# Eight matmuls on a zeroed tile first, the second chunk's moves on two queues, and the first two key tiles on one

## The chip, the core and the metric

The kernel runs on one core of a Trainium2 chip. The metric is the device time of the program in microseconds (us): before the change the median of three runs is 1068.44 us (1065.55 to 1068.86). Engines are named as in the profile: PE (TensorE matmuls; PEld its weight loads), DVE (VectorE), ACT (ScalarE), POOL (GpSimd), SP (SyncE). A "queue" is an engine that issues DMAs: here SP and ACT do.

## What is computed

An attention layer with talking heads, and two feed-forward layers behind it:

```python
scores = scale * np.matmul(q, k.transpose(0, 1, 3, 2))          # 4 batches, 12 heads, 448 x 448, depth 64
scores = np.einsum('bhij,hg->bgij', scores, w_pre)              # mix of the heads
scores = scores - np.max(scores, axis=-1, keepdims=True)
attn = np.exp(scores)
attn = attn / (np.sum(attn, axis=-1, keepdims=True) + 1e-09)
attn = np.einsum('bhij,hg->bgij', attn, w_post)                 # mix of the heads again
x = np.matmul(attn, v)                                          # then 1792 tokens of 768
h = x @ w_in                                                    # 768 -> 2048, ELU, -> 768
...
h = x @ w_in                                                    # 768 -> 1024, softmax * h, norm, -> 768
```

## The kernel before

The attention is worked off in chunks of query rows. The rows of a batch are cut into chunks of up to 12 groups of ten rows; the first batch has chunks of 6, 6, 12, 12 and 9 groups (`CH`), called chunk 0, 1, 2 and so on here. A chunk passes these steps:

1. **Scores** (`add_half` for chunks 0 and 1, L448; `add_score` for the others, L495): PE multiplies query tiles `q` and key tiles `kt` into PSUM tiles `sc`. One key tile holds two heads, so the six tiles of a batch are numbered by h = 0, 2, ..., 10. In chunks 0 and 1 a group of four matmuls takes two key tiles: h = 0 and 2, then 4 and 6, then 8 and 10.
2. **Evacuation** (`evac`, L454 and L501): ACT or DVE copies `sc` into SBUF: into tiles `s` of their own for chunk 0, into a ring of eight tiles `sev` for the others.
3. **Moves** (`move`, issued at L417): DMAs inside SBUF put the rows of a head into a tile `sp` in which head and row stand as the head mix needs them: ten rows of `sp` per move, for the last head twice five. A chunk has 13 moves. A move carries 105 KB in a chunk of 6 groups and 210 KB in one of 12.
4. **Units** of two groups: `pre` (L572) mixes the heads, out of `sp` into two PSUM tiles `pm` of a ring of three; DVE takes the maximum (L577), ACT the exponential (L582), POOL scales the second mix (L593), and `post` (L605) does the second mix with 56 small matmuls into `po`; a copy goes to `at`.
5. **Times the values** (L654, `av`), in two halves per chunk, and a store.

Units 0 to 2 belong to chunk 0, 3 to 5 to chunk 1, 6 to 11 to chunk 2. The first `pre` of a chunk waits for all 13 moves of it.

The order of the instructions on each engine isn't written out. `op` records every step with a rank (about when it is due, in planned us) and a planned duration for each engine that may do it, and `schedule()` puts the steps in order, engine by engine, and picks the engine for a step that lists several. So a move that lists `sp` and `act` may be issued by either queue, and any change of a rank or a duration can shift steps on all engines up to the end of the attention. Each engine then runs its own list in order: an instruction that waits holds up all behind it, a DMA issue on ACT's list included. All DMAs of both queues share eight semaphores in turn, so that a new one is issued only when the one eight places before it has landed.

Two feed-forward layers follow (from about 350 us on): L260 and L807, then L912 and L979.

Of the kernel before, what the change touches and what calls it, by code (L numbers as in the profile page):

```python
# [9 lines left out]
F32 = mybir.dt.float32  # L10
# [55 lines left out]
def kernel(ctx: ExitStack, tc: tile.TileContext, qa, kt, vt, wpre, wpost,  # L66
# [4 lines left out]
    nc = tc.nc  # L71
# [3 lines left out]
    def pool(name, bufs=1, side="left", space=None):  # L75
        kw = {"space": space} if space is not None else {"side": side}
        p = tc.alloc_tile_pool(name=name, bufs=bufs, reuse_waits="tile", **kw)
        pools[name] = p
        return p
# [48 lines left out]
    const = pool("const")  # L128
# [13 lines left out]
    ps_pm = pool("ps_pm", 3, space=PSUM)  # L142
# [152 lines left out]
    def op(rank, emit, deps=(), new=(), uses=(), more=0.0, lag=None, port=False, **us):  # L295

        o = Op()
        o.port = port
        o.rank, o.emit, o.deps, o.new, o.us, o.more, o.lag = rank, emit, [d for d in deps if d is not None], new, us, more, lag
        for b in chain(new, uses):  # L300
            b.users.append(o)
        ops.append(o)
        return o
# [67 lines left out]
    def copier(e):  # L371
        return nc.scalar.copy if e == "act" else nc.vector.tensor_copy
# [39 lines left out]
    kt_t, kb, q_t, qb_, sp_t, sp_op, pre_op, e_t = {}, {}, {}, {}, {}, {}, {}, {}  # L412
    po_t, ps_t, st_t, wr_t, v_t, x_t, at_t, T = {}, {}, {}, {}, {}, {}, {}, {}
    k_op, q_op, av_op, sc_ev = {}, {}, {}, {}

    def dma(out, in_, e="sp"):
        {"act": nc.scalar, "pool": nc.gpsimd, "sp": nc.sync}[e].dma_start(out=out, in_=in_)  # L417
# [2 lines left out]
    pool("spb")  # L420
    k0 = pool("k0")

    def add_q(c, hf):

        qb_[c, hf] = Buf("q")
        r = t_sc[c, 6 * hf]

        def load(e):
            q_t[c, hf] = q_p.tile([128, 3, 128], F32, tag="q", name="q")
            dma(q_t[c, hf], qa[c, :, 3 * hf:3 * hf + 3])  # L430

        q_op[c, hf] = op(r - 9 if c > 1 else 6.2 if c else [0.0, 3.0][hf], load, [], [qb_[c, hf]], sp=.5, more=.5)

    def add_half(c, n):

        b, _, G = CH[c]
        ring = ("sc", "pm")[n % 2] if c == 0 else "sc"
        scb, svb = [Buf(ring) for _ in range(2)], [Buf("sev") for _ in range(2)]
        r = t_sc[c, 4 * n]
        key = "sc", c, n  # L440

        def mm(e):
            T[key] = [pools["ps_" + ring].tile([128, 512], F32, tag=ring, name="sc") for _ in range(2)]
            q = q_t[c, 0].rearrange("p k n -> p (k n)")
            for x in range(2):
                for i in range(2):
                    sl, o = slice(64 * i, 64 * i + 64), 64 * (2 * n + x)
                    nc.tensor.matmul(T[key][i][64 * x:64 * x + 64, :S], q[sl, o:o + 64], kt_t[b, 4 * n + 2 * x][sl, :],  # L448
                                     start=True, stop=True)

        def evac(e, i):
            t = T["sv", c, n, i] = (k0.tile([128, S], F32, name=f"s0_{n}{i}") if c == 0 else
                                    sev_p.tile([128, S], F32, tag="sev", name="sev"))
            copier(e)(t, T[key][i][:, :S])  # L454

        def move(e, i, x, p, r0, r1):
            dma(sp_t[c][p:p + 13 * (r1 - r0 - 1) + 1:13, 0:G, :], T["sv", c, n, i][64 * x + r0 * G:64 * x + r1 * G], e)

        o1 = op(r, mm, [k_op[b, 4 * n], k_op[b, 4 * n + 2], q_op[c, 0]], scb, [qb_[c, 0], kb[b, 4 * n], kb[b, 4 * n + 2]], pe=SC)
        for i in range(2):  # L460
            sv = [] if c == 0 else [svb[i]]
            o2 = op(r + .9 + .1 * i, lambda e, i=i: evac(e, i), [o1], sv, [scb[i]], act=.43, dve=.54)
            for x in range(2):
                h = 4 * n + 2 * x + i
                for k, to in enumerate([(h, 0, 10)] if h < 11 else [(11, 0, 5), (64, 5, 10)]):
                    sp_op.setdefault(c, []).append(op(r + 2 + .2 * i + .1 * x + .05 * k, lambda e, i=i, x=x, to=to: move(e, i, x, *to),
                                                      [o2, o_clear.get(c)], [spb_[c]], sv, lag=3.5, sp=.78, **({'act': .78} if c == 0 else {})))

    def add_k(b, h):

        kb[b, h] = Buf("k")

        def load(e):
            kt_t[b, h] = k_p.tile([128, S], F32, tag="k", name="kt")
            dma(kt_t[b, h], kt[b, h // 2], e)

        r0 = t_sc[HEAD[b] - 1, h] if b else 0.0
        k_op[b, h] = op(r0 - 4 if b else .5 + h * .1 if h < 8 else 6.0 + h * .01, load, [], [kb[b, h]], lag=3.0, **{"sp" if b or h % 4 == 0 else "act": .5})

    def add_score(c, h):  # L480

# [33 lines left out]
    spb_ = {c: Buf(f"sp{(NC - c) % 3}") for c in range(NC)}  # L515
# [8 lines left out]
    def clear(t, us, r):  # L524
        return op(r, lambda e: nc.gpsimd.memset(t, 0.0), pool=us)
# [3 lines left out]
    o_clear = {c + 3: clear(sp_t[c][:, CH[c][2]:], .38 * (NH - CH[c][2]), 4.0 + c) for c in range(2)}  # L529
# [10 lines left out]
    for c in range(NC):  # L540
        b = CH[c][0]
        if c == HEAD[b]:
            for h in range(0, NH, 2):
                add_k(b, h)
        if c in HALF:
            add_q(c, 0)
            for n in range(3):
                add_half(c, n)
            continue
        for hf in range(2):  # L550
            add_q(c, hf)
        for h in range(0, NH, 2):
            add_score(c, h)
# [5 lines left out]
    for u, sl in enumerate(units):  # L559
# [56 lines left out]
        r0 = t_pre[u]  # L616
# [8 lines left out]
        r0 = t_post[u]  # L625
# [6 lines left out]
    for c in range(NC):  # L632
        b = CH[c][0]
# [270 lines left out]
    def hid2(t):  # L904
        h, lo = x2_t.pop(t)
        ps = ps_h2.tile([128, F2], F32, tag="h2", name="h2")
        for hf in range(2):
            n = 0
            for k in range(ECH):
                wh, wl = wi_t[k, hf]  # L910
                for a, w in ((h, wh), (lo, wh), (h, wl)):
                    nc.tensor.matmul(ps[:, hf * 512:hf * 512 + 512], a[:, k, :], w, start=n == 0, stop=n == 3 * ECH - 1)  # L912
                    n += 1
            spend(3.9)
        return ps
# [78 lines left out]
    for t in range(NTT):  # L994
        ps = hid2(t)
# [85 lines left out]
```

## Time and profile before

| | |
|---|---|
| median of three runs | 1068.44 us |
| profiled execution | 1073.62 us |
| span of it, first to last instruction | 1071.7 us |
| PE busy | 1043.1 us (97%) |
| DVE, ACT, POOL busy | 738.0, 499.9, 235.6 us |
| bytes moved by DMA | 153.86 MB |
| granted PE clock, mean | 0.992 |

Busy time is the time in which an engine has an instruction under way. PE is the engine that is nearly always busy, so what matters is where it isn't, and where its clock is at the lower of its two levels. In the tables by stretch, "PEclk" is the granted clock as a share of the full one, and "DMA share" is the mean busy share of the core's 16 DMA engines.

### The profile page before, as it was taken

The numbers are of one execution on the slowest core, as the hardware profiler recorded it, in microseconds if no ns is written. First come the engines' busy times: TensorE is split into PE (matmuls) and PEld (weight loads), VectorE is DVE, ScalarE is ACT, GpSimd is POOL, SyncE is SP. The second block draws the span as 40 slices with busy tenths as digits, with TensorE's granted clock in tenths as the row PEclk, the third lists the DMA queues.
The fourth block names the chain that finished last, engine by engine and source line by source line (L and its number), as shares of the span: only waits on it lengthen the run. The fifth ranks groups of instructions, "written<-read, shape, count | busy, mean of one in ns | idle before, by whom it ended". The sixth has DMA issues, their size and how long they took to land.

```text
span 1071.7 us, 28305 instructions
## 1 busy us (share of the span) xinstructions
PE 1043.1 (97%) x11656; PEld 881.8 (82%) x11656; DVE 738.0 (69%) x1396; ACT 499.9 (47%) x1063; POOL 235.6 (22%) x244
## 2 busy tenths in 40 slices
PE   7799999899899899999999999999999999999998
PEld 2567676667676799999999999999999898998988
DVE  5487877777586367698898888897964465545543
ACT  3376766676577365333333333343431343443423
POOL 4011111011013224343443334343433000000000
PEclk9899999999999999999999999999999999999999
DMA  6776776776845442414334242324162644243441
GB/s 202 222 210 213 224 215 198 213 217 205 223 130 175 134 130 79 157 60 161 115 118 153 84 157 79 128 74 142 50 235 99 255 95 108 70 94 75 88 109 45
DMA packets 132026, 153.86 MB, mean 144 GB/s; under 512 B 70745, under 2 KB 110393, under 8 KB 131897
## 3 DMA queue, kind: packets, MB, share of 16 engines
q1 hardware_dynamic: 129890, 148.95, 45.9%
q10 hardware_dynamic: 2006, 3.10, 0.9%
q8 instruction: 92, 1.51, 0.6%
q14 instruction: 38, 0.30, 0.1%
HBM read 81.86 MB, written 31.46 MB: 106 GB/s over the span
## 4 chain that ended last, share of the span: by engine, by line
PE 89%; DMA 4%; ACT 2%; issue 2%; DVE 2%; SPq 1%; DVEq 0%; ACTq 0%
PE o L807 22%; PE h L260 22%; PE o L979 11%; PE h L912 11%; PE av L654 6%; PE pm L572 6%; PE po L605 6%; PE sc L495 5%; DMA sp<-sev 2%; ACT e L582 1%; DVE st L577 1%; DMA q<-in_qa_dram 1%; DMA kt<-in_kt_dram 1%; ACT at L613 1%; SPq L417 1%
## 5 line engine op out<-in xcount | busy, mean ns | idle before, releaser
L577 DVE TENSOR_REDUCE st<-pm 128x1 f32<-128x448 f32 x180 | 105.4, 617 | 64.0 <-PE pm L572 61.9
L582 ACT ACTIVATE e<-pm,st 128x448 f32<-128x448 f32 x180 | 113.4, 635 | 60.6 <-DVE st L577 56.7
L807 PE MATMUL o<-gh,woh 128*128 128x448 f32 x384 | 140.5, 366 | 0.0
L605 PEld LDWEIGHTS po<-wr,e 60*64 60x64 f32 x5040 | 103.5, 136 | 44.6 <-issue 30.0
L807 PE MATMUL o<-glo,woh 128*128 128x448 f32 x384 | 140.0, 364 | 0.0
L807 PE MATMUL o<-gh,wol 128*128 128x448 f32 x384 | 139.5, 363 | 0.0
L979 PE MATMUL o<-w,lh 128*128 128x384 f32 x448 | 117.0, 338 | 0.0
L572 PE MATMUL pm<-sp,wpre_t 64*64 64x448 f32 x720 | 108.4, 567 | 7.6 <-DMA sp<-sev 3.1
L605 PE MATMUL po<-wr,e 60*64 60x60 f32 x5040 | 107.8, 221 | 7.9 <-issue 6.0
L495 PE MATMUL sc<-kt,q 64*64 64x448 f32 x720 | 107.5, 559 | 2.5 <-DMA q<-in_qa_dram 1.3
L823 DVE TENSOR_TENSOR x<-x,o 128x448 f32<-128x448 f32 x168 | 101.8, 610 | 11.2 <-PE o L807 10.6
L273 POOL TENSOR_TENSOR glo<-g,gh 128x448 fp32r<-128x448 f32 x64 | 80.2, 1254 | 132.8 <-ACT gh L272 111.9
L912 PE MATMUL h<-w,x2h 128*128 128x512 f32 x336 | 107.7, 395 | 0.0
L260 PE MATMUL h<-xh,wih 128*128 128x448 f32 x288 | 106.3, 369 | 0.0
L260 PE MATMUL h<-xh,wil 128*128 128x448 f32 x288 | 105.7, 367 | 0.0
L260 PE MATMUL h<-xl,wih 128*128 128x448 f32 x288 | 105.4, 366 | 0.0
L593 POOL TENSOR_TENSOR wr<-wpost_t,st 128x120 f32<-128x120 f32 x90 | 35.8, 398 | 293.0 <-DVE st L589 227.5
L276 ACT ACTIVATE t<-t 128x448 f32<-128x448 f32 x64 | 36.8, 575 | 109.0 <-DVE t L275 109.0
L654 PE MATMUL av<-at,v 128*64 128x120 f32 (+4 forms) x1632 | 82.0, 257 | 1.5 <-issue 1.0
L654 PEld LDWEIGHTS av<-at,v 128*64 128x64 f32 x1632 | 74.9, 137 | 10.0 <-issue 3.6
L979 PEld LDWEIGHTS o<-w,lh 128*128 128x128 f32 x448 | 81.8, 188 | 0.5
L807 PEld LDWEIGHTS o<-glo,woh 128*128 128x128 f32 x384 | 72.0, 187 | 6.1
(101 smaller groups left out, 1936.6 us busy)
## 6 DMA issues: line engine op xcount, KB each, us to landing
sp<-sev SPq DMA_DIRECT2D x92, 210.0 KB
ws<-in_wi_dram SPq DMA_DIRECT2D x33, 512.0 KB
ws<-in_wo_dram SPq DMA_DIRECT2D x21, 512.0 KB
q<-in_qa_dram SPq DMA_DIRECT2D x32, 192.0 KB
v<-in_vt_dram SPq DMA_DIRECT2D x24, 256.0 KB
w2s<-ws SPq DMA_DIRECT2D x12, 512.0 KB
ws<-in_wo_dram SPq DMA_DIRECT2D x16, 384.0 KB
w2s<-ws SPq DMA_DIRECT2D x16, 384.0 KB
```

The costliest lines, as they stand in the source:

```text
L260: nc.tensor.matmul(ps[:, :S], a[:, kc * FG + ft * 128:kc * FG + (ft + 1) * 128], x[:, kc, :], start=kc == 0 and n == 0, stop=kc == ECH - 1 ...
L273: nc.gpsimd.tensor_tensor(glo, g, f(gh), ALU.subtract)
L495: nc.tensor.matmul(T[key][i][64 * x:64 * x + 64, :S], q[sl, h % 6 // 2, 64 * x:64 * x + 64], k[sl, :], start=True, stop=True)
L572: nc.tensor.matmul(ps_t[u][r][64 * s:64 * s + 64, :S], wpre_t[p, :], sp_t[c][p, g, :], start=True, stop=True)
L577: nc.vector.tensor_reduce(out=st_t[u][:P, r:r + 1], in_=ps_t[u][r][:P, :S], op=ALU.max, axis=AX.X, negate=True)
L582: nc.scalar.activation(out=t[:P], in_=ps_t[u][r][:P, :S], func=AF.Exp, bias=st[:P, r:r + 1], scale=1.0, accum_out=st[:P, 2 + r:3 + r])
L605: nc.tensor.matmul(out[:, :, 5 * r:5 * r + 5], e_t[u, r][sl, 64 * n:64 * n + 64], wr_t[u][sl, r].rearrange("p (g a) -> p g a", a=5), start ...
L654: nc.tensor.matmul(ps[64 * k:64 * k + 64, i, :], v_t[CH[c][0]][:, 6 * n + 2 * i + k, q, :], at_t[c][:, q, 6 * n + 2 * i + k, :w], start=q ...
L807: nc.tensor.matmul(ps[:, :S], a[:, ft * DM + e * 128:ft * DM + (e + 1) * 128], x, start=n == 0, stop=n == 5)
L823: nc.vector.tensor_tensor(x1[tb][:, e, :], x1[tb][:, e, :], ps[:, :S], ALU.add)
L912: nc.tensor.matmul(ps[:, hf * 512:hf * 512 + 512], a[:, k, :], w, start=n == 0, stop=n == 3 * ECH - 1)
L979: nc.tensor.matmul(ps[:, :384], a[:, k, :], w, start=n == 0, stop=n == 3 * FC - 1)
```

## The change

Three edits. (1) A tile `idle` of 128 x 128 zeros is written by POOL ahead of its other work, and PE gets a first step of eight matmuls of it with itself into a `pm` tile that nobody reads. (2) The moves of chunk 1 may be issued by ACT as well as SP; so far that held for chunks 0 and 2. (3) Of the first batch's key tiles SP loads h = 0, 2 and 6, and ACT 4, 8 and 10, where SP loaded 0, 4 and 8 and ACT 2, 6 and 10; the ranks of the tiles 8 and 10 go from 6.08 and 6.10 to 1.3 and 1.5.

```diff
@@ -420,6 +420,16 @@
     pool("spb")
     k0 = pool("k0")
 
+    idle = const.tile([128, 128], F32, name="idle")
+    nc.gpsimd.memset(idle, 0.0)
+
+    def warm(e):
+        ps = ps_pm.tile([128, 512], F32, tag="pm", name="warm")
+        for i in range(8):
+            nc.tensor.matmul(ps[:, :128], idle, idle, start=True, stop=True)
+
+    op(0.0, warm, [], [Buf("pm")], pe=3.0)
+
@@ -464,7 +474,7 @@
                 for k, to in enumerate([(h, 0, 10)] if h < 11 else [(11, 0, 5), (64, 5, 10)]):
                     sp_op.setdefault(c, []).append(op(r + 2 + .2 * i + .1 * x + .05 * k, lambda e, i=i, x=x, to=to: move(e, i, x, *to),
-                                                      [o2, o_clear.get(c)], [spb_[c]], sv, lag=3.5, sp=.78, **({'act': .78} if c == 0 else {})))
+                                                      [o2, o_clear.get(c)], [spb_[c]], sv, lag=3.5, sp=.78, act=.78))
@@ -475,7 +485,7 @@
         r0 = t_sc[HEAD[b] - 1, h] if b else 0.0
-        k_op[b, h] = op(r0 - 4 if b else .5 + h * .1 if h < 8 else 6.0 + h * .01, load, [], [kb[b, h]], lag=3.0, **{"sp" if b or h % 4 == 0 else "act": .5})
+        k_op[b, h] = op(r0 - 4 if b else .5 + h * .1, load, [], [kb[b, h]], lag=3.0, **{"sp" if b or h in (0, 2, 6) else "act": .5})
```

What it does to the lists of the engines, at three places. Lines below L420 are ten higher in the changed kernel (L505 is L495 of before, and so on), and tile numbers differ. First SP's list from its start. Before, `kt_157`, `kt_161` and `kt_167` are h = 0, 4 and 8 (ACT loads 2, 6 and 10 as its first three steps):

```order
L417 DMA q_153<-in_qa_dram 128x384
L417 DMA kt_157<-in_kt_dram 128x448
L417 DMA kt_161<-in_kt_dram 128x448
L417 DMA q_165<-in_qa_dram 128x384
L417 DMA kt_167<-in_kt_dram 128x448
L417 DMA q_169<-in_qa_dram 128x384
```

And in the changed kernel, where `kt_168`, `kt_172` and `kt_176` are h = 0, 2 and 6 (ACT loads 4, 8 and 10):

```order
L417 DMA q_164<-in_qa_dram 128x384
L417 DMA kt_168<-in_kt_dram 128x448
L417 DMA kt_172<-in_kt_dram 128x448
L417 DMA kt_176<-in_kt_dram 128x448
L417 DMA q_178<-in_qa_dram 128x384
```

Tile h = 2, which the first group of score matmuls takes, was ACT's first load and is SP's third now; h = 6, in the second group, was ACT's second and is SP's fourth.

Second, SP's and ACT's moves. `sp_147`, `sp_149` and `sp_151` are chunks 0, 1 and 2 before; SP's list there, from the last move of chunk 0 on:

```order
L417 DMA sp_147<-s0_21_211 5x6x448
L417 DMA sp_149<-sev_223 10x6x448 x2
L417 DMA sp_149<-sev_233 10x6x448 x2
...
L417 DMA sp_149<-sev_254 5x6x448 x2
L417 DMA sp_151<-sev_338 10x12x448
L417 DMA q_365<-in_qa_dram 128x384
L417 DMA v_396<-in_vt_dram 128x512
```

In the changed kernel `sp_149`, `sp_151` and `sp_153` are chunks 0, 1 and 2. ACT's list there, from its last move of chunk 0 to the first exponential:

```order
L417 DMA sp_149<-s0_21_222 5x6x448
L464 COPY sev_252<-sc_238 128x448
L417 DMA sp_151<-sev_244 10x6x448
L417 DMA sp_151<-sev_250 10x6x448
L464 COPY sev_274<-sc_257 128x448
L417 DMA sp_151<-sev_252 10x6x448
L417 DMA sp_151<-sev_265 10x6x448
L417 DMA sp_151<-sev_274 10x6x448
L417 DMA sp_151<-sev_274 5x6x448
L592 ACTIVATE e_322,st_317<-pm_301,st_317 128x448
```

Six of the 13 moves of chunk 1 have gone to ACT, ahead of its first exponential; SP keeps seven. Of chunk 2's moves SP issues nine instead of five, ACT four instead of eight. The loads of `q` (two) and `v` (five) that stand on SP's list ahead of the last move of chunk 2 are the same number in both kernels.

Third, PE's list where chunk 2 begins (unit 6). Before, unit 6 is the first to read `sp_151`:

```order
L572 MATMUL pm_591<-sp_149,wpre_t_110 64x448
...
L495 MATMUL sc_602<-kt_161,q_365 64x448
...
L605 MATMUL po1_137<-wr_612,e_585 64x12x5
L654 MATMUL av_651<-at_414,v_396 64x60 x24
L572 MATMUL pm_686<-sp_151,wpre_t_110 64x448
```

In the changed kernel it is the first to read `sp_153`:

```order
L582 MATMUL pm_569<-sp_151,wpre_t_110 64x448
...
L615 MATMUL po1_137<-wr_554,e_502 64x12x5
L505 MATMUL sc_631<-kt_176,q_380 64x448
...
L582 MATMUL pm_645<-sp_153,wpre_t_110 64x448
...
L615 MATMUL po1_137<-wr_623,e_565 64x12x5
...
L664 MATMUL av_699<-at_445,v_366 64x60 x24
```

The `post` of unit 4 (56 matmuls) and the first half of `av` stood ahead of unit 6's `pre` and stand behind it now; one more group of four score matmuls stands ahead of it. Behind this place the lists of all engines differ in many small places up to the end of the attention, and are the same in the feed-forward layers but for their beginning.

## Rows read from the trace of the kernel before

**Rows 1.** The page: busy time, share of the span and instructions of each engine

```profile
PE 1043.1 (97%) x11656; PEld 881.8 (82%) x11656; DVE 738.0 (69%) x1396; ACT 499.9 (47%) x1063; POOL 235.6 (22%) x244
```

**Rows 2.** Table by stretch, the whole span

```profile
core 0: us, PE busy (x) PEld busy (x) DVE busy (x) ACT busy (x) POOL busy (x), PEclk, DMA share, GB/s
0.00:50.00 50.00, 37.27 (x520) 18.33 (x524) 27.41 (x55) 17.42 (x43) 13.94 (x14) 0.90 0.70 212
50.00:400.00 350.00, 337.48 (x7826) 250.16 (x7820) 244.63 (x591) 232.64 (x599) 51.83 (x98) 0.99 0.65 191
400.00:1071.00 671.00, 668.32 (x3320) 613.34 (x3319) 465.95 (x751) 249.79 (x424) 169.86 (x132) 1.00 0.37 114
```

**Rows 3.** PE in order of time: start, us, [idle before <- releaser]

```profile
5.22 6.90 PE L448 MATMUL sc<-kt,q 64*64 64x448 f32 x34 [5.22 <-DMA kt<-in_kt_dram]
...
30.54 2.36 PE L572 MATMUL pm<-sp,wpre_t 64*64 64x448 f32 x5 [3.06 <-DMA sp<-sev]
...
46.86 1.78 PE L572 MATMUL pm<-sp,wpre_t 64*64 64x448 f32 x8 [2.02 <-issue]
```

**Rows 4.** Line 448, up to 9.0 us and after: ns min/median/max

```profile
L448 PE MATMUL sc<-kt,q x21: 851/951/1007, 5.2 to 9.0; 64*64 64x448 f32 x21
...
L448 PE MATMUL sc<-kt,q x28: 536/587/851, 9.0 to 14.5; 64*64 64x448 f32 x28
```

**Rows 5.** The chain that ended last: start us, us, what

```profile
1.19 3.90 DMA kt<-in_kt_dram
...
39.54 5.29 DMA sp<-sev
44.84 2.02 issue
46.86 1.78 PE pm L572 x8
48.64 1.25 PE sc L495 x6
49.89 1.30 PE po L605 x53
...
52.74 0.91 PE pm L572 x8
53.65 0.75 PE sc L495 x8
54.40 0.81 PE po L605 x56
55.22 1.54 PE av L654 x48
```

**Rows 6.** Table by stretch, 9 to 46.8 us, columns as above

```profile
9.00:18.00 9.00, 8.05 (x46) 2.11 (x42) 4.99 (x10) 1.50 (x3) 3.15 (x2) 1.00 0.56 178
18.00:30.00 12.00, 8.57 (x166) 4.01 (x158) 8.60 (x20) 5.85 (x16) 1.16 (x3) 1.00 0.62 184
30.00:38.00 8.00, 7.46 (x89) 4.46 (x90) 3.22 (x7) 2.15 (x6) 0.00 (x0) 0.57 0.92 252
38.00:46.80 8.80, 6.26 (x188) 4.05 (x183) 5.11 (x13) 5.49 (x15) 1.16 (x3) 1.00 0.68 205
```

**Rows 7.** All engines in order of time, 0 to 31 us

```profile
0.73 6.86 POOL L522 MEMSET sp<- 128x2688 f32 x2 [0.29 <-POOLq L1070]
...
6.28 0.20 PEld L448 LDWEIGHTS sc<-kt,q 64*64 64x64 f32 x4 [0.76 <-DMA kt<-in_kt_dram]
...
7.06 0.53 ACT L454 COPY s<-sc 128x448 f32<-128x448 f32 x1 [3.63 <-PE sc L448]
...
7.63 6.98 ACTq L417 DMA_DIRECT2D sp<-s  x7
...
13.32 15.51 SPq L417 DMA_DIRECT2D sp<-sev  x14
...
19.36 0.63 ACT L582 ACTIVATE e<-pm,st 128x448 f32<-128x448 f32 x1 [2.14 <-DVE st L577]
```

## The prediction

> **What bounds the kernel now.** The page gives PE 97% of the span [rows 1], so I looked first at where the missing 3% are. The table by stretch shows 12.7 us without a matmul in the first 50 us (50 less 37.27), 12.5 us in the 350 us up to 400 (350 less 337.48), and 2.7 us in all the rest [rows 2]. The change works on the first 50 us. PE in order of time shows three waits there: 5.22 us for the first key tiles, 3.06 us up to 30.54 for chunk 1's moves, and 2.02 us up to 46.86 at the first head mix of chunk 2 (unit 6) [rows 3]. The third is put down to "issue", but the chain reaches it through one of chunk 2's last moves, which landed at 44.84 [rows 5]; the other half of the last head is issued right behind it, so I read the 2.02 us as that half still on its way. From 46.86 on the chain is PE without a break as far as the rows go [rows 5]. So the end of the front, as I call 46.86 us, is the time to follow: what comes before it counts only if it brings that time forward.
>
> What sets it? The table by stretch from 9 to 46.8 us shows the DMA engines at a share of 0.56, 0.62, 0.92 and 0.68, with 178, 184, 252 and 205 GB/s [rows 6]. Between 18 and 30 us, while both queues do nothing but moves, it stays at 0.62 although SP has an issue under way nearly all the time (14 in 15.51 us [rows 7]) and ACT issues moves of chunk 2 beside it. 0.62 of 16 engines is 10, and a move writes ten rows. The step to 0.92 comes with the loads of `v` and `q`, which write 128 rows. I take it that a move uses ten of the sixteen engines, the same ten as every other move, and that these ten are full from 12 us on. Then the front ends when the bytes ahead of chunk 2's last move have gone through, in whatever order they go.
>
> The Trainium skill says both halves of this. "DMA: Bandwidth & Descriptors", section "Why a DMA increments its semaphore by 16 and not by 1", has a DMA use the largest number of engines up to 16 that divides the slowest dimension on both sides, ten here and always the lowest-numbered ten. Its section "Issuing engines are not separate DMA queues" has a second issuing engine save only issue time. The share of 0.62 agrees with the first; for the second the trace has ACT and SP issuing side by side from 18 to 30 us at no higher rate than 184 GB/s [rows 6]. By these rules the second edit can't make the moves of the front faster as a whole, and the sum below would be the same.
>
> **Part by part.**
>
> *Eight matmuls of zeros.* No row has a 128 x 128 by 128 fp32 matmul. Nearest: in the first 4 us of line 448 a 448-column pass of four small matmuls at once is 951 ns long as recorded, 587 ns later, when the clock is up [rows 4]. An fp32 matmul appears as two passes there. Eight times two passes of 128 columns, each 128/448 of 951 or 587 ns: 4.3 us or 2.7 us. POOL's zeros cost it 128/8064 of its first 6.86 us (two tiles, 2688 and 5376 columns [rows 7]), 0.1 us. POOL starts at 0.73 [rows 7], so the eight run from about 0.9 us to between 3.6 and 5.2. The key tiles come at 5.1 (1.19 and 3.90 of the chain [rows 5]): the cost is 0 to 0.1 us, and I take 0, as PE has nothing else to do before. The gain: the durations show a low clock up to between 9.0 and 9.7 us, so it rose some 4 us after PE began at 5.22 [rows 3, 4]. If it is up at about 6 instead, the three groups of chunk 0 come out faster. But ACT's seven moves of chunk 0 take 6.98 us from 7.63 on, nearly one after another [rows 7], so what counts of it is only the first evacuation, at 7.06.
>
> *Key tiles.* The first group of matmuls takes h = 0 and h = 2. h = 0 keeps its place, but h = 2 goes from ACT's first load to SP's second key. What stood there landed at about 6.25: the second group's weight load waited up to 6.28 for a key tile [rows 7]. So half of the first group starts 1.1 us later than 5.22. At the full clock a group of four takes 0.75 us (53.65 [rows 5]), and half a group no less, as the four run side by side: the first evacuation starts at 7.1 to 7.2, where it was 7.06, and nothing is lost. With a clock still low the half takes 1.5 us, and the evacuation starts at about 8.2 (after 5.22 and twice 1.5): 1.1 us lost, and all moves with it. I take 0.1, on account of the eight matmuls. So the first edit only pays for the third.
>
> *Chunk 1 on both queues.* Chunk 1's bytes now go ahead of chunk 2's instead of beside them. A chunk of 6 groups has 12 x 60 rows of 448 fp32, 1.29 MB. By 18 us 9 x 178 = 1.60 MB had gone; the 2.58 MB of chunks 0 and 1 are through 0.98 / 184 = 5.3 us later, at 23 to 25 us instead of 30.5. The 3.06 us wait and the low clock behind it (0.57 over 30 to 38 [rows 6]) go. But ACT's first exponential, at 19.36 [rows 7], now stands behind six more issues; seven took 6.98 us from 7.63 [rows 7], so behind its seven of chunk 0 the six run to about 20.5: chunk 0's units are 1 us later, which is hidden as long as chunk 2's data is late.
>
> What is late next is chunk 2. By 46.8 us 1.60 + 2.21 + 2.02 + 1.80 = 7.63 MB had gone [rows 6]. Needed for unit 6 are 5.16 MB of moves (1.29, 1.29 and 2.58), two `q` (0.39) and five `v` (1.31): 6.86 MB, and the same loads stand ahead of the last move of chunk 2 in the changed list. 0.77 MB had slipped past, which at 205 GB/s is 3.8 us. So unit 6 can start between 43.1 us (nothing slips past) and 46.9 (as now). I take 45.0: gain 1.9 us, range 0 to 3.8.
>
> *The order at unit 6.* PE now meets unit 6's `pre` before the `post` of unit 4 and the first half of `av`, and has one more score group behind it. So work that covered the wait stands behind it: 0.81 + 1.54 - 0.75 = 1.6 us lost [rows 5]. PE also gets to that place earlier (about 36 us) and waits up to 9 us, against 2. After the 2 us wait the next `pre`, score group and `post` took 1.78, 1.25 and 1.30 us against 0.91, 0.75 and 0.81, 1.9 us lost on the low clock [rows 5]; after the 3 us wait at 30.54 a mean of 0.57 over 8 us says up to 3.4 [rows 6]. So 0 to 1.5 us more; I take 0.5.
>
> *Behind the front.* The order of all engines differs in many places up to 400 us. It changes no work, but the 12.5 us without a matmul there [rows 2] can come out otherwise. Nothing says which way: 0, range -4 to +4.
>
> **Sum** on the profiled execution: 1073.62 + 0.1 - 1.9 + 1.6 + 0.5 = 1073.9 us, its span being 1071.7 and 1.9 around it. That execution was 5.2 us above the median of the runs, so at the median 1068.44 + 0.3 = 1068.7 us.
>
> **Rivals.**
>
> *A, faster: chunk 2 doesn't wait for the ten engines.* If the moves of chunk 1 and 2 were held by issue and not by bytes, unit 6 would start when PE gets there: chunk 1 at 24 instead of 30.5, then 14.3 us of PE (30.54 to 44.84), less 3.1 for the clock: 35.2. That is 11.7 less 1.6, some 10 us: 1058.5. For it: SP is busy issuing. Against: the share stays at 0.62 [rows 6]. A weaker form has nothing slip past (43.1), the clock no worse and 2 to 3 us less waiting behind the front: -3.8 + 1.6 - 2.5, 1063.7.
>
> *B, slower: the clock is still low when the keys come.* Then the first evacuation and every move behind it is 1.1 us later; the ten engines carry that to unit 6, the 0.77 MB slip past as now, and the loss on order and clock stays: 1.1 + 1.6 + 1.5 = 4.2, 1072.6. It decides where the first score group ends after 8 us. For it: the zeros and the keys are 0 to 1.5 us apart, and the clock rose only 4 us after PE's start. A worse order behind the front ends at the same time.
>
> *C: nothing is gained by the eight matmuls, and nothing lost by the keys*, because SP and ACT issue chunk 0's moves at the same pace: 1068.5, inside the forecast.
>
> **How the numbers follow.** A measurement of this kernel tells 0.3%, 3.2 us, from no change. The forecast with C has 0.47, the two forms of A 0.05 and 0.20, B and the worse order 0.28. Hence faster 0.26, same 0.46, slower 0.28. The forecast's own range is 1066 to 1071; 8 in 10 reaches into the weaker A and past B: 1063.5 to 1073.5.
>
> **What would show it.** Right: eight matmuls before 5 us; the first evacuation near 7.1; no wait for chunk 1 near 24 us, and in its place one wait of 6 to 9 us at unit 6, up to 43 to 47; a DMA share near 0.62 while only moves run. Wrong: a share well above 0.65 there, or unit 6 before 42 us (A); the first evacuation after 8 us (B); or waits behind 50 us that differ by more than 4 us.

## The result, and the profile after

| | before | after |
|---|---|---|
| median, side by side (22 runs each) | 1067.72 us | 1072.99 us |
| profiled execution | 1073.62 us | 1079.98 us |
| its span | 1071.7 us | 1078.2 us |

The ratio after to before is 1.0053, with a 95% interval of 1.003 to 1.0076: the change makes the kernel slower by 0.5%, some 5.7 us. (The medians are of all 22 runs; the ratio leaves out one run of after, 1082.83 us at a lower granted clock.) The forecast was 1068.7 us, or 0.3 us more than before; 1072.99 lies inside its range of 1063.5 to 1073.5, half a microsecond from its upper end. Both profiled executions lie above the medians of their kernels, by 5.9 us before and 7.0 us after.

The page of after, its first row, for [rows 1], and the table by stretch, for [rows 2]:

```profile
PE 1046.7 (97%) x11672; PEld 882.7 (82%) x11672; DVE 737.8 (68%) x1400; ACT 497.9 (46%) x1058; POOL 239.2 (22%) x246
```

```profile
0.00:50.00 50.00, 36.23 (x441) 17.82 (x443) 26.01 (x53) 16.52 (x40) 14.09 (x15) 0.97 0.65 203
50.00:400.00 350.00, 336.04 (x7894) 245.91 (x7889) 242.62 (x592) 226.53 (x586) 53.87 (x98) 0.99 0.64 190
400.00:1078.00 678.00, 674.38 (x3350) 618.99 (x3349) 469.18 (x756) 254.83 (x432) 171.26 (x134) 1.00 0.37 114
```

PE is without a matmul for 13.8 us in the first stretch and 14.0 in the second. Before it was 12.7 and 12.5, but of its 12.7 us 5.22 lay ahead of the first score matmul, where after has its eight matmuls of zeros. Counted from the first score matmul to the last matmul, all gaps sum to 20.0 us before and 26.1 us after. That is the 6.1 us by which the last matmul of the profiled execution ends later (1068.3 and 1074.4 us from the start). From the first matmul of line 807 (817 after, the expert's output) on, both take 689.5 us, so all that this pair of executions differs by is lost ahead of it.

PE of after in order of time, for [rows 3] and the first waits behind:

```profile
0.99 3.79 PE L429 MATMUL warm<-idle 128*128 128x128 f32 x16 [0.99 <-POOL idle L424]
5.40 5.06 PE L458 MATMUL sc<-kt,q 64*64 64x448 f32 x26 [0.62 <-DMA kt<-in_kt_dram]
...
18.33 1.25 PE L582 MATMUL pm<-sp,wpre_t 64*64 64x448 f32 x5 [0.43 <-DMA sp<-sev]
...
29.13 1.11 PE L582 MATMUL pm<-sp,wpre_t 64*64 64x448 f32 x8
...
46.48 2.71 PE L582 MATMUL pm<-sp,wpre_t 64*64 64x448 f32 x5 [4.98 <-DMA v<-in_vt_dram]
48.29 0.65 PE L615 MATMUL po<-wr,e 60*64 60x60 f32 x4
48.94 0.99 PE L582 MATMUL pm<-sp,wpre_t 64*64 64x448 f32 x3
...
52.84 1.91 PE L664 MATMUL av<-at,v 128*64 128x60 f32 x48
54.69 0.98 PE L582 MATMUL pm<-sp,wpre_t 64*64 64x448 f32 x8
...
145.64 1.77 PE L505 MATMUL sc<-kt,q 64*64 64x448 f32 x8 [3.72 <-DMA q<-in_qa_dram]
```

The wait for chunk 1 at unit 3 is gone (29.13 without a bracket, where before had 3.06 us up to 30.54). In its place stands one wait of 4.98 us at unit 6, and behind it `post`, a score group and half an `av`, so unit 7 starts at 54.69; before, it started at 52.67. The score group that waits 3.72 us for a `q` tile at 145.64 waits less before:

```profile
134.65 0.98 PE L495 MATMUL sc<-kt,q 64*64 64x448 f32 x8 [1.31 <-DMA q<-in_qa_dram]
```

The chain around unit 6, for [rows 5]:

```profile
42.63 5.40 DMA sp<-sev
48.03 0.14 issue
48.16 0.46 PE pm L582
```

The second half of the last head's move lands at 48.03. So 46.48 is only where the first matmul of unit 6 starts (two of its eight records, at 46.48 and 47.08); the other six start from 48.16 on, three of them at 48.94. Before, all eight start from 46.86 on without a pause. "DMA v" in the row above is only what landed last by the profile at 46.48.

The table by stretch, for [rows 6]:

```profile
9.00:18.00 9.00, 6.40 (x42) 1.59 (x35) 4.77 (x10) 0.53 (x1) 3.29 (x2) 1.00 0.50 159
18.00:30.00 12.00, 9.18 (x121) 4.05 (x125) 7.85 (x18) 6.04 (x17) 0.78 (x2) 1.00 0.61 187
30.00:38.00 8.00, 6.59 (x157) 3.84 (x150) 6.07 (x15) 4.46 (x13) 0.78 (x2) 1.00 0.72 222
38.00:46.50 8.50, 3.31 (x76) 1.61 (x71) 2.80 (x8) 3.14 (x8) 0.78 (x2) 1.00 0.68 196
```

With chunk 1's moves on both queues the share from 18 to 30 us is 0.61 at 187 GB/s; with chunk 1's on SP and chunk 2's on ACT beside them it was 0.62 at 184. From 9 to 18 us and from 30 to 38 us the DMA engines carry less than before (159 against 178 GB/s, 222 against 252): by 46.5 us 7.12 MB have gone, where before 7.63 had by 46.8. Line 458 up to 9.0 us and behind 9.3, for [rows 4], and the first rows of ScalarE and GpSimd, for [rows 7]:

```profile
L458 PE MATMUL sc<-kt,q x18: 766/951/1003, 5.4 to 8.8; 64*64 64x448 f32 x18
...
L458 PE MATMUL sc<-kt,q x34: 536/537/917, 8.4 to 15.0; 64*64 64x448 f32 x34
...
8.04 0.53 ACT L464 COPY s<-sc 128x448 f32<-128x448 f32 x1 [4.61 <-PE sc L458]
...
0.73 0.21 POOL L424 MEMSET idle<- 128x128 f32 x1 [0.29 <-POOLq L1080]
0.87 6.86 POOL L532 MEMSET sp<- 128x2688 f32 x2
```

In this execution the score matmuls were still at 951 ns up to 9 us, as without the eight, and the first evacuation came at 8.04 instead of 7.06. That is rival B's start. Whether it is its cause too, the experiments had to say.

### The profile page after: what moved, and what is told of

It is laid out like the page before. It is cut to its first block, busy times and chain, and to the rows that moved or that the text cites. A ratio compares the mean times of both kernels' runs of the same rounds, so it can differ in the third digit from the quotient of the medians.

```text
span 1078.2 us, 28354 instructions
## 1 busy us (share of the span) xinstructions
PE 1046.7 (97%) x11672; PEld 882.7 (82%) x11672; DVE 737.8 (68%) x1400; ACT 497.9 (46%) x1058; POOL 239.2 (22%) x246
## 4 chain that ended last, share of the span: by engine, by line
PE 91%; DMA 4%; issue 2%; ACT 1%; DVE 1%; SPq 0%; DVEq 0%; ACTq 0%
PE o L817 22%; PE h L260 22%; PE o L989 11%; PE h L922 11%; PE av L664 7%; PE po L615 7%; PE pm L582 6%; PE sc L505 5%; DMA sp<-sev 2%; DMA q<-in_qa_dram 1%; DMA sp<-s 1%; ACT e L592 1%; DVE st L587 1%; SPq L417 0%; DMA kt<-in_kt_dram 0%
## 5 line engine op out<-in xcount | busy, mean ns | idle before, releaser
L505 PE MATMUL sc<-kt,q 64*64 64x448 f32 x720 | 104.5, 556 | 7.6 <-DMA q<-in_qa_dram 4.7
```

The costliest lines, as they stand in the source:

```text
L505: nc.tensor.matmul(T[key][i][64 * x:64 * x + 64, :S], q[sl, h % 6 // 2, 64 * x:64 * x + 64], k[sl, :], start=True, stop=True)
```

## The experiments

Two things changed at once: what is emitted (matmuls, queues of the moves, queues of the keys), and the order that the planner makes for every engine because its options changed. The first four runs part them. All ratios are to before, with 95% intervals.

**The edits in before's order.** The eight matmuls alone (`e1_warm`), the second edit alone (`e2_moves`), and all three (`e5_all3`), each put in where it is emitted, so that the planner knows nothing of it. (Seven of chunk 1's 13 moves go to ACT here; in the changed kernel the planner gives it six.)

```diff
+    idle = const.tile([128, 128], F32, name="idle")
+    nc.gpsimd.memset(idle, 0.0)
+    ps = ps_pm.tile([128, 512], F32, tag="pm", name="warm")
+    for i in range(8):
+        nc.tensor.matmul(ps[:, :128], idle, idle, start=True, stop=True)
...
-            dma(sp_t[c][p:p + 13 * (r1 - r0 - 1) + 1:13, 0:G, :], T["sv", c, n, i][64 * x + r0 * G:64 * x + r1 * G], e)
+            dma(sp_t[c][p:p + 13 * (r1 - r0 - 1) + 1:13, 0:G, :], T["sv", c, n, i][64 * x + r0 * G:64 * x + r1 * G], "act" if c == 1 and x else e)
...
-            dma(kt_t[b, h], kt[b, h // 2], e)
+            dma(kt_t[b, h], kt[b, h // 2], "sp" if b or h in (0, 2, 6) else "act")
```

> Before with the eight matmuls on the zeroed tile alone; every engine's order is otherwise that of before. Theory 1 (what the change costs is the order that the planner makes of it, not the edits themselves): ratio to before 0.998 to 1.002; the matmuls end near 4.8 us, ahead of the first score matmul (5.2 to 5.4), the clock rises near 9.2 to 9.6 as in both traces, unit 6's pre starts at 46 to 48 us, end within 2 us of before. Rival B (what the edits do on the chip in the first 20 us delays every move): the first pre moves from 16.9 to about 18.3 us, everything behind it 1 to 1.4 us later, ratio 1.001 to 1.003. Rival W (the matmuls do warm the engine): clock high before 9 us, first pre at 16.0 or earlier, ratio 0.998 or less.

> Before's order on every compute engine; of the 13 moves of chunk 1, the 7 of the second key half are issued by ScalarE instead of SyncE. Theory 1: the 3.06 us wait ahead of unit 3's pre at 30.54 goes or shrinks below 1.5 us, but the bytes through ten engines are the same, so unit 6's pre stays at 45 to 47.5 us and the ratio is 0.997 to 1.002. Rival A (the issuing queue bounds the front end): unit 6's pre at 43.5 us or earlier and a ratio of 0.997 or less. Rival B (ScalarE's copies wait behind the DMA issues): unit 6's pre at 48 us or later, ratio 1.001 to 1.003.

> Before's order on TensorE, VectorE and GpSimd with all three edits in the code that is emitted (matmuls on the zeroed tile, seven moves of chunk 1 by ScalarE, the third key tile by SyncE instead of the fifth). Theory 1: ratio 0.997 to 1.002, unit 6's pre at 45 to 47.5 us, no wait of more than 0.5 us near 142 us. Rival B (the edits themselves cost): first pre near 18.3 us and a ratio of 1.003 to 1.007, as the changed kernel.

Measured (12 runs each): `e1_warm` 0.9974 (0.9948 to 1.0), `e2_moves` 0.9983 (0.9962 to 1.0005), `e5_all3` 0.9983 (0.9964 to 1.0002). None of the edits is seen to cost anything in before's order; if anything they give 0.2%. `e1_warm` falls between its rivals: the first evacuation comes early (6.75 us), as W has it, but the first `pre` doesn't (17.01 us, against 16.91 before).

**The order without the edits** (`e4_order`): the changed kernel, planned as it is, with the reverse of these three substitutions where it emits.

```diff
-        ps = ps_pm.tile([128, 512], F32, tag="pm", name="warm")
-        for i in range(8):
-            nc.tensor.matmul(ps[:, :128], idle, idle, start=True, stop=True)
+        pass
...
-            dma(sp_t[c][p:p + 13 * (r1 - r0 - 1) + 1:13, 0:G, :], T["sv", c, n, i][64 * x + r0 * G:64 * x + r1 * G], e)
+            dma(sp_t[c][p:p + 13 * (r1 - r0 - 1) + 1:13, 0:G, :], T["sv", c, n, i][64 * x + r0 * G:64 * x + r1 * G], "sp" if c == 1 else e)
...
-            dma(kt_t[b, h], kt[b, h // 2], e)
+            dma(kt_t[b, h], kt[b, h // 2], "sp" if b or h % 4 == 0 else "act")
```

> The changed kernel's order on TensorE, VectorE and GpSimd, without the three edits: no matmuls on the zeroed tile, chunk 1's moves all by SyncE, key tiles on the queues of before. Theory 1: ratio to before 1.003 to 1.008, with unit 6's pre at 46 to 48 us, work behind that wait that before has ahead of it (about 2.4 us), and a wait of 2 us or more near 142 us. Rival B (the edits themselves cost): ratio 0.998 to 1.002.

Measured: 1.0109 (1.0081 to 1.0136), from 4 runs. It is slower than the theory's bound, and unit 6 comes at 55.04 where 46 to 48 was expected. I put that down to an order that counts on moves and keys which come later here, but no run shows it apart:

```profile
43.07 2.12 PE L613 MATMUL po<-wr,e 60*64 60x60 f32 x53 [3.65 <-DVE at L621]
...
55.04 2.04 PE L580 MATMUL pm<-sp,wpre_t 64*64 64x448 f32 x5 [4.64 <-DMA sp<-sev]
```

So the loss comes with the order: it needs none of what the edits do, and the edits without it don't lose. That all three edits are no slower in before's order speaks against rival B; the late first evacuation by itself is in `p3_keys`, next.

**Which edit makes the order?** Each edit as in the change, planner included: the second alone (`p2_moves`), the third alone (`p3_keys`), both (`p23`). (The matmuls alone leave the planner's order of every engine as it was, so `e1_warm` is the first edit alone.) The diff is that of `p23`; `p2_moves` has its first pair of lines, `p3_keys` its second.

```diff
-                                                      [o2, o_clear.get(c)], [spb_[c]], sv, lag=3.5, sp=.78, **({'act': .78} if c == 0 else {})))
+                                                      [o2, o_clear.get(c)], [spb_[c]], sv, lag=3.5, sp=.78, act=.78))
...
-        k_op[b, h] = op(r0 - 4 if b else .5 + h * .1 if h < 8 else 6.0 + h * .01, load, [], [kb[b, h]], lag=3.0, **{"sp" if b or h % 4 == 0 else "act": .5})
+        k_op[b, h] = op(r0 - 4 if b else .5 + h * .1, load, [], [kb[b, h]], lag=3.0, **{"sp" if b or h in (0, 2, 6) else "act": .5})
```

> The change's second edit alone, told to the planner: chunk 1's moves may be issued by ScalarE, and the planner lays out everything anew for it (e2_moves had the two queues in before's order). Theory 1, sharpened by the first four runs (the loss is the new order, and the new order comes from this edit): ratio to before 1.003 to 1.009, idle time of TensorE between 10 and 60 us 2 us or more above before's 8.2, since pre matmuls stand earlier in the order than their moves land. Rival P (the key edit's plan makes the loss): ratio 0.997 to 1.002.

> The change's third edit alone, told to the planner: third key tile on SyncE instead of the fifth, and its ranks. TensorE's order differs from before in under 500 places of 7578, none in the first 50 us. Theory 1: ratio 0.997 to 1.003. Rival P: 1.003 to 1.008.

> The changed kernel without the eight matmuls on the zeroed tile; its order on every engine is else that of the changed kernel. Theory 1: the matmuls are worth what they were in before's order (e1_warm 0.9974 of before), so this is 0.1 to 0.4 per cent slower than the changed kernel: ratio to before 1.006 to 1.010. Rival (they are worth nothing): 1.004 to 1.006. Rival (they cost, by the first pre at 18.3 us in the changed kernel): 1.003 or less.

Measured: `p2_moves` 0.9982 (0.9961 to 1.0003), `p3_keys` 1.0018 (0.9997 to 1.0039), `p23` 1.0073 (1.0045 to 1.0102; 6 runs). My sharpened theory, that the second edit's order loses, is wrong: that order is different from before on every engine and no slower. Of the orders tried, only that of both edits together is slow. PE's order of the two in the front, units in brackets:

```
p2_moves: pre[4] post[2] sc post[3] pre[5] sc post[4] pre[6] sc av pre[7]
p23:      pre[4] post[2] sc pre[5] sc post[3] sc pre[6] post[4] sc av pre[7]
```

**Unit 6 put back** (`f1_late6`): the changed kernel, its plan recorded first and emitted with unit 6's `pre`, and what follows from it, moved behind `post` of unit 4, the score group and the half of `av`.

```diff
-            o.emit(e)
+            plan.append((o, e))
...
+        back = [x for x in plan[:stop] if x[0] in late]
+        plan = [x for x in plan[:stop] if x[0] not in late] + back + plan[stop:]
+        for o, e in plan:
+            o.emit(e)
```

> The changed kernel with one thing moved: unit 6's pre and what follows from it (maxima, exponentials, weights) stand behind unit 4's post, one score group and half of an av product, just ahead of unit 7's pre. Theory 1 (work that could have filled the wait stands behind it): the wait of 4.98 us at 41.5 shrinks by the 2.4 to 2.6 us of work put ahead of it, unit 7's pre starts 2 us or more earlier than 54.69, ratio to before 1.001 to 1.004. Rival Q (the front is not what counts: its loss is given back behind, or the loss is made near 142 us): ratio 1.004 to 1.007 as the changed kernel.

Measured: 1.0062 (1.0036 to 1.0088), no better than the changed kernel.

```profile
43.79 0.96 PE L516 MATMUL sc<-kt,q 64*64 64x448 f32 x2 [2.46 <-DVE sev L522]
46.12 1.77 PE L516 MATMUL sc<-kt,q 64*64 64x448 f32 x6 [1.36 <-ACT sev L522]
47.81 2.82 PE L675 MATMUL av<-at,v 128*64 128x60 f32 x48
50.56 2.53 PE L593 MATMUL pm<-sp,wpre_t 64*64 64x448 f32 x10
```

The wait did shrink, from 4.98 to 2.46 and 1.36 us in front of a score group, and unit 7 came at 52.11 instead of 54.69, the 2.6 us that were expected. The whole kernel is no faster for it. So this one swap isn't where the loss is settled.

**Front or back?** The planner runs twice in one kernel, with the key edit and without it, and two plans are spliced at unit 24's `pre` (about 110 us). `h1_newfront` has the changed kernel's order up to there and the other behind; `h2_newback` the reverse; `p12` is the other plan all through, that is, the change without its key edit. Below is `h1_newfront`; `h2_newback` has the two plans the other way round.

```diff
+        front, back = plans[1], plans[0]
+        n = next(i for i, (o, _) in enumerate(front) if o is pre_op[24]) + 1
+        seen = {o for o, _ in front[:n]}
+        for o, e in front[:n] + [x for x in back if x[0] not in seen]:
+            o.eng = e
+            o.emit(e)
```

> The planner runs twice, with the changed kernel's key edit and without it; emitted are the changed kernel's instructions up to unit 24's pre (about 115 us), then the rest in the order of the plan without the key edit. All three edits' front end is there. Theory K (the loss is made behind the front, by the order that the key edit brings from about 110 us on, with its wait for q near 142 us): ratio to before 0.997 to 1.002, no wait above 1 us between 135 and 150 us. Theory F (the loss is made in the first 60 us, by a pre that stands ahead of a post): ratio 1.004 to 1.008, as the changed kernel.

> The reverse: up to unit 24's pre the plan without the key edit, from there the changed kernel's order. Theory K: ratio 1.003 to 1.008 with a wait for q above 1 us between 135 and 150 us. Theory F: ratio 0.996 to 1.002.

> The change without its key edit: matmuls on the zeroed tile, and chunk 1's moves planned on both queues; its order is that of p2_moves with eight matmuls ahead. Both theories: what p2_moves (0.9982) and e1_warm (0.9974) gave, 0.995 to 0.999, the fastest version so far. Against it: if ratios below 1 were only spread, 0.998 to 1.001.

Measured (12 runs each): `p12` 0.9984 (0.9957 to 1.001), `h1_newfront` 1.0022 (0.9998 to 1.0047), `h2_newback` 1.0007 (0.9982 to 1.0033). Neither theory K nor F holds alone: against `p12` the new front costs 0.38%, the new back 0.23%, together 0.61%, and the changed kernel, which has both, lies 0.69% above `p12`. The sum fits. By the twelve runs of each the front's half is 4.2 us, with a 95% interval of 2.5 us either way, and the back's is 2.5 us, no more than its own of 2.6. The traces make the front's half firmer. PE at units 6 and 7 of `p12`, then of `h1_newfront`:

```profile
45.23 2.13 PE L582 MATMUL pm<-sp,wpre_t 64*64 64x448 f32 x8 [6.83 <-DMA sp<-sev]
...
48.76 1.62 PE L664 MATMUL av<-at,v 128*64 128x60 f32 x48
50.30 0.98 PE L582 MATMUL pm<-sp,wpre_t 64*64 64x448 f32 x8
```

```profile
46.08 2.39 PE L601 MATMUL pm<-sp,wpre_t 64*64 64x448 f32 x5 [4.97 <-DMA v<-in_vt_dram]
48.22 1.00 PE L601 MATMUL pm<-sp,wpre_t 64*64 64x448 f32 x3
...
51.43 1.61 PE L683 MATMUL av<-at,v 128*64 128x60 f32 x48
52.98 0.98 PE L601 MATMUL pm<-sp,wpre_t 64*64 64x448 f32 x8
```

`p12` waits longer at unit 6 (6.83 us) and is ahead at unit 7. It has `post` of unit 4 behind it already, and its data comes earlier: all of unit 6 runs from 45.23 on, while in `h1_newfront` six of the eight records start from 47.45 on, and in after from 48.16. SP's list shows a part of the reason. First after, then `p12`; chunk 2's last two moves are the row "x2" in after, and the last two of the row "x3" in `p12`:

```profile
39.63 0.78 SPq L417 DMA_DIRECT2D sp<-sev  x1
40.45 1.19 SPq L417 DMA_DIRECT2D v<-in_vt_dram  x1
41.75 1.64 SPq L417 DMA_DIRECT2D sp<-sev  x2
```

```profile
38.40 2.49 SPq L417 DMA_DIRECT2D sp<-sev  x3
40.94 0.56 SPq L417 DMA_DIRECT2D v<-in_vt_dram  x1
```

With the key edit the planner puts one more load of `v` ahead of these two moves, and SP is through with them at 43.39 instead of 40.89. 1.2 us of these 2.5 were there one move earlier (39.63 against 38.40). `p23`, `f1_late6` and `h1_newfront` have the load at this place too. `p3_keys`, at 1.0018, has it too. No run moves this load alone, so what it costs isn't shown.

To compare places across orders I count PE's lag: how much later than in `p12` a unit's `pre` starts, less the matmuls that PE has done more by then, at their full-clock time from [rows 5] (0.91, 0.75, 0.81 and 1.54 us for a `pre`, a score group, a `post` and half an `av`; the matmuls of the hidden layer, a few of which come early, at 0.20 us each). One profiled execution each, in us:

| kernel | unit 7 | unit 24 | unit 35 | line 807's first matmul |
|---|---|---|---|---|
| before | 0.0 | -0.2 | 2.3 | 8.2 |
| `p12` | 0 | 0 | 0 | 0 |
| `p2_moves` | 1.7 | 1.2 | 2.6 | 0.5 |
| `e5_all3` | -2.1 | -0.9 | 0.6 | -2.1 |
| after | 3.6 | 6.1 | 14.1 | 14.3 |
| `p23` | 3.1 | 6.0 | 12.1 | 11.0 |
| `f1_late6` | 1.1 | 4.6 | 9.2 | 7.0 |
| `h1_newfront` | 1.9 | 5.0 | 8.4 | 5.1 |
| `h2_newback` | 0.0 | -0.6 | 2.9 | -1.5 |

The four kernels with the new front and the edits are 4.6 to 6.1 us behind at unit 24, the others of the table within 1.2 (not listed: `e4_order` 12.4, `e1_warm` 2.1, `p3_keys` 2.0, `e2_moves` 1.1). The last column doesn't rank the kernels: it is of one execution each, and those stand up to 7 us off the medians. (`h2_newback` was profiled at 1064.23, 5.9 us below its median, and is 2.5 us slower than `p12` by the runs, not 1.5 us ahead.) 2.5 to 3.5 us of the lag at unit 24 are made between units 7 and 24. There the other engines do less in the same time: the stretch from 56 to 115 us, of before, `p12`, after and `h1_newfront`:

```profile
56.00:115.00 59.00, 58.21 (x1464) 40.41 (x1462) 46.16 (x120) 42.09 (x113) 6.69 (x17) 1.00 0.71 213
```

```profile
56.00:115.00 59.00, 58.58 (x1529) 42.49 (x1525) 46.41 (x120) 41.89 (x113) 6.19 (x16) 1.00 0.70 209
```

```profile
56.00:115.00 59.00, 57.53 (x1490) 42.25 (x1481) 42.30 (x110) 39.58 (x106) 5.81 (x15) 1.00 0.64 184
```

```profile
56.00:115.00 59.00, 56.74 (x1474) 41.64 (x1472) 41.57 (x110) 39.40 (x107) 5.97 (x16) 1.00 0.63 185
```

VectorE is busy for 42 us instead of 46, with 110 instructions instead of 120, and the DMA engines move 184 instead of 210 GB/s. Whether that is the cause of the lag or the lag itself, seen from the other engines, isn't shown; which instruction starts it is open.

Behind unit 24 the new order meets `q` later than `p12` does. `p23` and `h2_newback`:

```profile
143.72 1.77 PE L495 MATMUL sc<-kt,q 64*64 64x448 f32 x8 [2.79 <-DMA q<-in_qa_dram]
```

```profile
135.99 0.98 PE L524 MATMUL sc<-kt,q 64*64 64x448 f32 x8 [1.64 <-DMA q<-in_qa_dram]
```

After has 3.72 us at this place, `f1_late6` 1.29, `h1_newfront` and `p12` none above 1 us between 100 and 150 us. So against `p12` this wait goes with the new back. But it isn't new: before has 1.31 us there. After and `p23`, the longest, have both the late front and the new back, and `f1_late6` has them too with 1.29, so one execution each doesn't say what sets its length.

## Why the prediction was right, and where its terms were off

The time was forecast at before plus 0.3 us; it is plus 5.7 us by the ratio, on the slower side of a range that holds it by 0.5 us. That it does is owed to the width of the range, and so in part to luck: the range reached up to there for rival B, which isn't what happened, and the one gain in the sum came out as a loss. Step by step:

- **Ten engines set the pace of the moves: right.** 0.61 at 187 GB/s from 18 to 30 us with chunk 1's moves on two queues, 0.62 and 184 with them on one. The rows give a mean share, not which engines were busy, so the ten are still read from it. The equal rate agrees with what the Trainium skill says in "DMA: Bandwidth & Descriptors", section "Issuing engines are not separate DMA queues", that a second issuing engine saves issue time alone. Rival A falls with it: `e2_moves`, with the two queues in before's order, has the same time as before within 0.4%, and unit 6 at 46.9.
- **Chunk 1's wait goes, one wait at unit 6 comes: right.** 3.06 us are gone and unit 6 waits 4.98 us, and again for its last six records; 6 to 9 was forecast.
- **Chunk 2's data, -1.9: it came later, not earlier.** This is the term that failed first. Six of the eight records of unit 6 start from 48.16 on, where before all ran from 46.86: a loss of 1.3 us where the sum has a gain, with a range of 0 to 3.8. The late first evacuation of this execution has a share in it, but in `h1_newfront`, which has it at 7.32, they start from 47.45 on, also later than before. I let the bytes ahead of chunk 2's last move go as fast as before. In after the DMA engines carried less (7.12 MB by 46.5 us, against 7.63 by 46.8), and the last move landed at 48.03. Part of that is when SP comes to issue the last moves, as the rows of its list above suggest; no run shows it alone. Without the key edit unit 6 started at 45.23 (`p12`), near the 45.0 forecast.
- **The key tiles: right to 0.3 us, both ways.** The first evacuation was forecast at 7.1 to 7.2 with the clock up (7.21 to 7.32 came) and at about 8.2 with it low (7.94 to 8.06 came). The row of `e5_all3` and that of `p3_keys`, the key edit without the eight matmuls:

```profile
7.21 0.53 ACT L460 COPY s<-sc 128x448 f32<-128x448 f32 x1 [1.48 <-PE sc L454]
```

```profile
8.06 0.53 ACT L454 COPY s<-sc 128x448 f32<-128x448 f32 x1 [4.63 <-PE sc L448]
```

- **The eight matmuls bring the clock up early: right as a rule, not in the profiled execution.** Without the key edit they bring the first evacuation to 6.32 us (`p12`), and score matmuls are at 537 ns from 5.3 us on:

```profile
L458 PE MATMUL sc<-kt,q x26: 536/537/588, 5.3 to 8.9; 64*64 64x448 f32 x26
...
6.32 0.53 ACT L464 COPY s<-sc 128x448 f32<-128x448 f32 x1 [2.88 <-PE sc L458]
```

  So it was in six of the seven profiled executions that have the eight matmuls: the first evacuation at 6.32, 6.35 and 6.75 where it is 6.93 to 7.06 without them (`e4_order` apart, whose first key tile came 0.9 us later), and with the key edit at 7.21, 7.28 and 7.32 where it is 7.94 and 8.06. The profile of after is the seventh, with 8.04. The Trainium skill says in "TensorE: Matmul & The Clock Gate", section "Part 1: The HAM clock gate", that the number of matmuls that run before the clock rises varies from run to run of one kernel; one late rise among these seven fits it, but they are one execution each of seven kernels, so no run here shows it of one kernel. The early clock is worth little: from `p23` to after 0.2%, from before to `e1_warm` 0.26%, the first within the uncertainty, the second at its edge.
- **The order at unit 6, +1.6 and +0.5: about right up to unit 7, too small behind it.** Against before, after has lost 3.6 us by unit 7 where the sum has 0.3 (0.1 - 1.9 + 1.6 + 0.5); with the +1.3 of chunk 2's data in place of the -1.9 it has 3.5. By unit 24 it is 6.3 us (6.1 and -0.2 in the table). I counted what stands behind the wait and put nothing down for what follows it. But the lag grows for another 60 us, in which VectorE and the DMA engines do less than in `p12`.
- **Behind the front, 0 with a range of -4 to +4: the other half.** Splicing puts the new back at 0.23% (2.5 us) on a good front. In the pair of profiles it is plus 5.5 us from unit 24 to 35 (14.1 - 6.1 less 2.3 + 0.2), and minus 5.7 us from there to line 807, where before had waits of its own. One execution each, so these two are no more than a hint.
- **Rival B: its time, not its mechanism.** 1072.6 was its price and 1072.99 the result. But the late first evacuation is at most a small part of the cause: `p3_keys` has it at 8.06 too and is at 1.0018. Of the executions with the new front, the two with an early one (`f1_late6` 7.28, `h1_newfront` 7.32) still lag by 4.6 and 5.0 us at unit 24; the two with a late one (`p23` 7.94, after 8.04) by 6.0 and 6.1. That is about the 1.1 us that B gave it. The remark beside it, that a worse order behind the front would end at the same time, is what happened, with the front itself in it.

Open: what the `v` load ahead of chunk 2's last moves costs, which instruction of the new front starts the lag of units 7 to 24, and why the planner's order with both edits is bad where each alone is not. No version that was tried is surely faster than before: `e1_warm`, `e2_moves`, `e5_all3`, `p2_moves` and `p12` lie at 0.9974 to 0.9984, each with an interval that reaches 1. Against the changed kernel `p12`, which only leaves out the key edit, is 0.7% faster.

## What to carry to other kernels

Where a planner sets the order, an edit is two changes: run it once in the old order and once with the new order alone, before the edit itself is blamed or praised. The length of a wait doesn't price it (6.83 us in `p12` went with a faster kernel than 4.98 us in after): look at when its data comes and at what could have run but is queued behind it. Bytes counted at the old rate don't say when data is there (1.3 us late here, where a gain of 1.9 was forecast), so see also what the issuing queue now puts ahead of the last transfer. Here the lag grew by 2.5 to 3.5 us behind the first wait: follow it for several units past the wait before pricing it.

## What was not expected of the hardware

- The clock fell at the same wait in both, but at different cost. In `p12` the mean granted clock (1.00 is 2.4 GHz, the lower level of 1.2 GHz is 0.50) is 0.79 from 36 to 46 us, where PE is busy for 3.17 us, and 0.87 from 46 to 56. In after it is 1.00 and then 0.66, with PE busy for 9.39 us: it fell about when the first matmul of unit 6 started, and most of the low clock lay on work. What set the moment isn't known.

```profile
36.00:46.00 10.00, 3.17 (x82) 2.38 (x76) 3.25 (x8) 2.88 (x8) 0.77 (x2) 0.79 0.59 176
46.00:56.00 10.00, 10.00 (x210) 6.49 (x205) 5.59 (x14) 4.21 (x12) 0.77 (x2) 0.87 0.76 228
```

```profile
36.00:46.00 10.00, 5.28 (x112) 2.58 (x102) 4.56 (x11) 5.03 (x13) 1.16 (x3) 1.00 0.70 203
46.00:56.00 10.00, 9.39 (x136) 5.26 (x140) 3.46 (x8) 3.15 (x8) 0.39 (x1) 0.66 0.67 216
```

- From the first matmul of line 807 to the last matmul, 12 of the 13 profiled executions took 689.5 us, and `p12` 690.1, while the time ahead of it ran from 368.5 to 386.7 us: nearly all of the spread between kernels and executions lies in the attention part.
